# A gated feed-forward kernel with a convolution in front: phases of three rounds in place of two

## The chip, the cores and the metric

The kernel runs on one core of a Trainium2 chip. A core has five engines that run side by side, each with its own queue of instructions, taken in order: TensorE (PE in the profile; PEld is its loading of weights), VectorE (DVE), ScalarE (ACT), GpSimd (POOL) and SyncE (SP), which here only issues transfers. Transfers run on 16 DMA engines, which are shared by a hardware queue (fed by SyncE) and a software queue (fed by GpSimd). SBUF is the working memory. PSUM holds the results of matmuls; the kernel uses it as four buffers of two banks, taken in turn.

The metric is the time of one execution on the device in microseconds (us), as the median of several runs.

## The reference

The input `x` has 8 sequences of 3904 tokens with 192 channels. First comes a causal convolution with 7 taps, separately for each channel: the 192 channels form 8 heads of 24, and all channels of a head share the head's taps, a softmax over `weight[h, :]`. The result, seen as 31232 tokens of 192 channels, goes through a feed-forward block:

```
a = x @ w1          # 192 -> 1024
b = x @ w2          # 192 -> 1024
h = (a * b) @ w3    # 1024 -> 1024
out = h @ w_out     # 1024 -> 192
```

There is no nonlinearity after the product `a * b`, so `w3 @ w_out` is one matrix of 1024 x 192, which the kernel computes once.

## The kernel before

**Rounds.** The tokens are two halves of 15616 (`NS = 2`, `r` = 0 and 1). A round `R` is 512 tokens of each half; there are 31 rounds (0 to 30), the last 256 wide. `first_product(R)` computes for each of 8 f-tiles (128 of the 1024 columns) `pa = x w1` and `pb = x w2` of both halves: six pairs of matmuls, a pair being the two halves on the two halves of the array's rows. ScalarE copies `pa` to SBUF (L564), VectorE multiplies with `pb` (L566) and writes `abT`. `second_product(R, r)` multiplies `abT` by the combined 1024 x 192 matrix (32 matmuls, L582); ScalarE copies the result to a slot `osb` (L587), and SyncE sends it out (L592), 384 KB. `abT` has three buffers.

**Phases.** After a beginning with the first products of rounds 0, 1 and 2, the loop at L795 walks over phases. Phase 0 has no first products; phase p has those of rounds 2p+1 and 2p+2, and then the four second products of rounds 2p and 2p+1. One round is thus always left over, and the last phase has three rounds of second products. All engines' instructions are in the order of this program; nothing is reordered later.

**The convolution** is done in two ways.
- By TensorE, for most rounds: windows of 32 rows of `x` (`xb`, loaded by GpSimd in `x_jobs`, L157) are multiplied by a band matrix (`conv`, L323); the results are evicted (L332), stored to a table `rows` in DRAM (`store`, L354 and L361, on SyncE), and read back by DMA transposes into a ring `xT` of four rounds (`transposes`, L395, on SyncE). This goes by batches of windows; batch 4 covers rounds 5 and 6, batch 5 rounds 9 to 12, batch 6 rounds 17 to 20, batch 7 rounds 25 to 28. A batch is cut into units (`units`: two for batch 4, four for each later one), and `places` says after which of a phase's second products a unit is put.
- By VectorE for the six round pairs in `SIDE` (rounds 7 and 8, 13 and 14, 15 and 16, 21 and 22, 23 and 24, 29 and 30): GpSimd casts the raw channels into a table `rows_c` (`side_cast`, L439), SyncE transposes them (`side_transpose`, L449), ScalarE scales by one tap (`side_first`, L455), and VectorE adds the six others one after another (`side_sums`, L473), writing `side`. A task is 64 channels of a round pair; a step of a task is a unit, and a unit is two instructions where a sequence begins inside the pair. `room` says how many units a phase takes. Two tasks are given to GpSimd in steps (`pool_sums`, L500 to L520).

**Pacing.** GpSimd's loads and steps in a phase stand in `jobs` and `pool_at`; they are put at `points`, pairs of a round's number in the phase and an f-tile. At a point GpSimd first copies two elements of that f-tile's `abT` (L805), and so waits for VectorE.

**SyncE's order around phase 0 and 1:** transposes for sums of the next phase, outputs, the store of a batch when its last unit is done, outputs, and at the end of a phase the transposes into the ring for rounds whose batch is stored (`due`, at most two rounds a phase).

Of the kernel before, what the change touches and what calls it, by code (L numbers as in the profile page):

```python
# [9 lines left out]
BF16 = mybir.dt.bfloat16  # L10
# [6 lines left out]
def kernel(  # L17
# [19 lines left out]
    NS = 2  # L37
    TS = B * S // NS
    CH = 512
    NR = -(-TS // CH)  # L40
    RING = 4 * CH
    LAG = 2
    Q = 64
    NP = D // Q
    C = 32
# [6 lines left out]
    XN = 20 * D  # L52
# [14 lines left out]
    conv_rounds = [R for R in range(NR) if phase_of(R) not in SIDE]  # L67
# [22 lines left out]
    stage = ctx.enter_context(tc.tile_pool(name="stage", bufs=2))  # L90
    work = ctx.enter_context(tc.tile_pool(name="work", bufs=2))
# [8 lines left out]
        return psum.tile([128, 16, 128], BF16, tag="banks", name=name)  # L100

    def slot(shape, dtype, name):
        return stage.tile(shape, dtype, tag="slot", bufs=4, name=name)

    rows = dram.tile([TS, NP * NS * Q], BF16, name="rows")
    rows_c = dram.tile([TS, NP, NS * Q], BF16, name="rows_c")
# [29 lines left out]
    def x_jobs(b, part):  # L136
        js = parts_of(b)[part]
        n, m, E = shape_of(b)
        tiles = xb_of.setdefault(b, {})

        def alloc():
            xb = work.tile([128, XN], BF16, tag="xb", bufs=6, name="xb")
            xb = xb[:, 0:len(js) * m * D].rearrange("p (w d) -> p w d", d=D)
            for j in js:
                tiles[j] = (xb, (j - js[0]) * m)
                for e in range(E):
                    for u in range(m):
# [243 lines left out]
    def transposes(R, first=0):  # L391
        t0, t1 = max(R * CH, first), min((R + 1) * CH, TS)
        a = ring_of[R] * CH % RING + t0 - R * CH
        for k in range(NP):
            nc.sync.dma_start_transpose(  # L395
                out=xT[k][:, a:a + t1 - t0], in_=rows[t0:t1, k * 128:(k + 1) * 128])
# [36 lines left out]
    def side_cast(i, task=None):  # L433
        p, k = task or tasks[i]
        t0, t1 = side_span(p)

        def job(r):
            def run():
                nc.gpsimd.dma_start(  # L439
                    out=rows_c[t0 - HALO:t1, k, r * Q:r * Q + Q],  # L440
                    in_=x_rows[r * TS + t0 - HALO:r * TS + t1, k * Q:k * Q + Q])
            return run
        return [job(r) for r in range(NS)]
# [232 lines left out]
        swap_w(k, HC + 256, DFF, P)  # L676
    load_w3(0, 4, range(2, 4))

    phases = [()] + [(R, R + 1) for R in range(LAG + 1, NR, 2)]
    assert phases[-1][-1] == NR - 1  # L680

    places = {0: (1, 2), 1: (2,), 2: (0, 1, 2), 5: (0, 2), 6: (0, 2), 9: (0, 2), 10: (0, 2)}
    starts, chain, room, p = {}, {}, 0, -1
    for i, (q, k) in enumerate(tasks):
        for cost, f in side_sums(i):
            while room < cost:
                p += 1
                room = 6 if p == 0 else 8 if len(places.get(p, ())) == 2 else 7
                at, ends = 0, {}
                starts.setdefault(p, [])  # L690
            if not chain or chain[max(chain)][-1][0] != i:
                starts[p].append(i)
                n = max(p == 0, -(-ends.get(i - 2, 0) // 2))
                chain.setdefault(p, []).append((i, n, lambda i=i: side_first(i)))
            assert p < q
            room, at = room - cost, at + cost
            chain.setdefault(p, []).append((i, None, f))
        ends[i] = at
# [23 lines left out]
    def later_loads():  # L722
        nc.gpsimd.tensor_scalar(out=taps, in0=taps, scalar1=total, scalar2=None, op0=ALU.mult)
        load_x(3)
        load_wo()
        load_w3(4, 2)
        load_w3(6, 2)
        for i in starts[0]:
            for f in side_cast(i):
                f()  # L730
        load_x(4)
        for i in starts[1]:
            for f in side_cast(i):
                f()
        for f in x_jobs(5, 0):
            f()

    first_product(0, {
        0: seq((swap_w, 1, 256, HC, A, (1,))),
# [19 lines left out]
             for n in [max(v for v in (2, 4) if v * shape_of(b)[1] * G <= CH)]  # L759
             for h in range(0, H, n)]  # L760
    assert sum(map(len, places.values())) == len(units)
    jobs = {p: [] for p in range(1, len(phases))}
    for p, b, part in ((1, 5, 1), (3, 6, 0), (4, 6, 1), (7, 7, 0), (8, 7, 1)):
        jobs[p] += x_jobs(b, part)
    pool_at = {3: 4, 4: 3, 5: 4, 6: 3, 7: 4, 8: 3, 9: 4, 10: 3}
    halves = [(q, k, h) for q, k in BY_POOL for h in range(2)]
    pool_sum = [f for v in halves for f in pool_sums(*v)]
    assert sum(pool_at.values()) == len(pool_sum)
    pool_from = {2: halves[0], 4: halves[1], 6: halves[2], 8: halves[3]}
    casts = [(p - 1, f) for p in starts if p > 1 for i in starts[p] for f in side_cast(i)]  # L770
    casts += [(p, f) for p, t in zip((2, 6), BY_POOL) for f in side_cast(None, t)]
    casts.sort(key=lambda c: c[0])
    for p in jobs:
        due_now = sum(d <= p for d, _ in casts)
        ahead = max(due_now, min(len(casts), 6 - len(jobs[p])))
        jobs[p] = ([f for _, f in casts[:due_now]] + jobs[p] +
                   [f for _, f in casts[due_now:ahead]])
        del casts[:ahead]
    points = ((0, 1), (0, 3), (0, 5), (0, 7), (1, 2), (1, 4))
    sent = [LAG + 3]  # L780
    due = []

# [8 lines left out]
                sent[0] += 1  # L791

    pace = const.tile([1, 2], BF16)
    done = 0
    for p, rounds in enumerate(phases):  # L795
        todo = jobs.pop(p, [])

        each = -(-len(todo) // len(points))
        at = [[todo.pop(0) for _ in range(min(each, len(todo)))] for _ in points]
        for v in {0: (), 2: (1, 4), 3: (0, 2, 4), 4: (0, 1, 3, 4)}[pool_at.get(p, 0)]:  # L800
# [12 lines left out]
        assert not todo  # L813
        for b in {u[0] for u in units[:3]}:
            for xb, p0, w in zero_rows.pop(b, []):
                nc.gpsimd.memset(xb[p0:p0 + PAD, w, :], 0.0)
        for i in starts.get(p + 1, ()):
            side_transpose(i)
        if p == 0:
            pool_tiles()  # L820
        if p in pool_from:
            pool_transpose(*pool_from[p])
        state = set()
        last = NR if p == len(phases) - 1 else done + 2
        seconds = [(R, r) for R in range(done, last) for r in range(NS)]
        done = last
        for n, (R, r) in enumerate(seconds):
            side_steps(p, n, state)
            (last_product if (R, r) == (NR - 1, NS - 1) else second_product)(R, r)
            if n in places.get(p, ()):  # L830
                convolve(p)
        assert len(state) == len(chain.get(p, ()))
        for R in due[:2]:
            transposes(R)
        del due[:2]
    assert not pool_sum and not units and not due and not jobs and done == NR and sent[0] == len(conv_rounds)


# [28 lines left out]
```

## Time and profile before

| | |
|---|---|
| median of 3 runs | 514.11 us (513.78 to 514.99) |
| profiled execution | 514.66 us, span 513.0 us |
| TensorE busy | 506.8 us, 99% of the span |
| VectorE busy | 432.4 us, 84% |
| ScalarE busy | 351.6 us, 69% |
| GpSimd busy | 162.8 us, 32% |
| products on VectorE (L566) | 240 of 1221 ns |
| copies on ScalarE (L564) | 244 of 1012 ns |
| software queue (GpSimd) | 17.07 MB, 36.2% of 16 engines' span |
| hardware queue (SyncE) | 41.39 MB, 37.7% |

The page of a profile gives busy times and shares, the span in 40 slices, the chain of work that ended last, and the costliest groups of instructions. A line of a timeline gives start, duration, engine, source line, operation, tile and count; a bracket gives the idle time before it and what ended it. Durations of neighbouring instructions of one engine can overlap a little, so the distance between two starts is the better cost of one in a row.

### The profile page before, as it was taken

How to read it: one execution, taken by the hardware profiler on the slowest of the kernel's cores; microseconds unless marked ns; L12 is line 12 of the kernel's file. 1: busy time of each engine (PE TensorE's matmuls, PEld its weight loads, DVE VectorE, ACT ScalarE, POOL GpSimd, SP SyncE). 2: the span in 40 equal slices, each digit the busy share in tenths (PEclk: the TensorE clock that was granted, in tenths of full speed). 3: DMA queues.
4: the chain of work that ended last, by engine and by line, in shares of the span. 5: the costliest groups of instructions: out<-in, count | busy, mean ns of one | idle time of the engine just before them, and what ended most of it. 6: DMA issues, size and time to landing. Idle time of an engine off the chain costs nothing.

```text
span 513.0 us, 13921 instructions
## 1 busy us (share of the span) xinstructions
PE 506.8 (99%) x5892; PEld 332.9 (65%) x5892; DVE 432.4 (84%) x430; ACT 351.6 (69%) x397; POOL 162.8 (32%) x243
## 2 busy tenths in 40 slices
PE   8999999999999999999999999999999999999997
PEld 4446846757558585675856758567585675846777
DVE  7898779899798998989989899898998989877380
ACT  6886668677874757777787475777777757476562
POOL 9965031030480724708247072560500000000000
PEclk9999999999999999999999999999999999999999
DMA  9999999895898935956589893584028452210305
GB/s 144 146 162 171 166 110 228 126 175 95 142 193 172 138 80 82 86 145 44 94 152 175 184 139 76 98 48 141 1 64 145 115 148 42 70 57 1 124 3 155
DMA packets 154134, 59.45 MB, mean 116 GB/s; under 512 B 108891, under 2 KB 154071, under 8 KB 154071
## 3 DMA queue, kind: packets, MB, share of 16 engines
q1 hardware_dynamic: 86999, 41.39, 37.7%
q0 software_dynamic: 66912, 17.07, 36.2%
q8 instruction: 46, 0.75, 0.6%
q14 instruction: 17, 0.14, 0.1%
q10 hardware_dynamic: 160, 0.10, 0.1%
HBM read 34.42 MB, written 34.88 MB: 135 GB/s over the span
## 4 chain that ended last, share of the span: by engine, by line
PE 97%; DVE 1%; ACT 1%; issue 1%
PE ops L582 32%; PE pa L557 31%; PE pb L557 30%; PE cps L323 2%; PE wps L650 1%; PE warm L233 1%; ACT asb L564 1%; DVE abT L566 0%; ACT convo L332 0%; PE ops L603 0%; PE tps L385 0%; PE tps L370 0%; DVE xT L377 0%; DVE xb L277 0%; DVE Aband L287 0%
## 5 line engine op out<-in xcount | busy, mean ns | idle before, releaser
L566 DVE TENSOR_TENSOR abT<-asb,pb 128x1024 bf16<-128x1024 bf16 x240 | 292.7, 1221 | 56.7 <-ACT asb L564 41.5
L564 ACT CAST asb<-pa 128x1024 bf16<-128x1024 f32 x244 | 247.0, 1012 | 63.2 <-PE pa L557 62.8
L557 PEld LDWEIGHTS <-wn 64*128 64x128 bf16 x1488 | 138.1, 94 | 84.8 <-issue 2.2
L557 PEld LDWEIGHTS <-ws 64*128 64x128 bf16 x1488 | 130.9, 94 | 71.1 <-issue 0.5
L582 PE MATMUL ops<-W_sb,abT 128*128 128x192 bf16 x1936 | 164.9, 246 | 1.2 <-issue 1.2
L582 PEld LDWEIGHTS <-abT 128*128 128x128 bf16 x1936 | 158.2, 98 | 9.5 <-issue 9.4
L557 PE MATMUL pb<-xT,wn 64*128 64x512 bf16 x456 | 123.9, 376 | 0.0
L557 PE MATMUL pa<-xT,wn 64*128 64x512 bf16 x456 | 123.0, 376 | 0.2
L557 PE MATMUL pa<-xT,ws 64*128 64x512 bf16 x456 | 123.1, 376 | 0.0
L557 PE MATMUL pb<-xT,ws 64*128 64x512 bf16 x456 | 122.0, 376 | 0.0
L587 ACT COPY osb<-ops 128x768 f32<-128x768 f32 (+1 forms) x61 | 48.4, 793 | 86.3 <-PE ops L582 86.3
L473 DVE SCALAR_TENSOR_TENSOR acc<-raw,wC,acc 128x320 f32<-128x320 bf16 (+4 forms) x90 | 76.2, 894 | 0.7
L557 PE MATMUL pb<-side,wn 64*128 64x512 bf16 (+1 forms) x288 | 74.9, 367 | 0.0
L557 PE MATMUL pa<-side,ws 64*128 64x512 bf16 (+1 forms) x288 | 74.4, 367 | 0.0
L557 PE MATMUL pa<-side,wn 64*128 64x512 bf16 (+1 forms) x288 | 74.4, 367 | 0.0
L557 PE MATMUL pb<-side,ws 64*128 64x512 bf16 (+1 forms) x288 | 73.8, 367 | 0.0
L805 POOL COPY pace<-abT 1x2 bf16<-1x2 bf16 x55 | 9.6, 175 | 187.0 <-DVE abT L566 186.9
L500 POOL TENSOR_SCALAR tmp<-acc,wC 128x512 f32<-128x512 bf16 x24 | 37.6, 1568 | 0.8
L332 ACT CAST convo<-cps 128x640 bf16<-128x640 f32 (+2 forms) x58 | 33.8, 659 | 1.8 <-PE cps L323 1.7
L157 POOL DMA_DIRECT2D xb<-in_x_dram x46 | 31.0, 675 | 9.5 <-issue 4.8
L439 POOL DMA_DIRECT2D rows_c<-in_x_dram x36 | 28.5, 792 | 5.4 <-issue 4.4
L520 POOL TENSOR_TENSOR acc<-acc,tmp 128x512 f32<-128x512 f32 (+6 forms) x25 | 26.0, 1047 | 1.7
(72 smaller groups left out, 170.3 us busy)
## 6 DMA issues: line engine op xcount, KB each, us to landing
out_dram<-osb SPq DMA_DIRECT2D x54, 384.0 KB
xb<-in_x_dram POOLq DMA_DIRECT2D x28, 240.0 KB, 7.1
rows_c<-in_x_dram POOLq DMA_DIRECT2D x30, 130.0 KB, 4.1
out_dram<-osb SPq DMA_DIRECT2D x12, 192.0 KB
rows<-convo SPq DMA_DIRECT2D x9, 240.0 KB
xb<-in_x_dram POOLq DMA_DIRECT2D x8, 228.0 KB, 7.9
rows<-convo SPq DMA_DIRECT2D x9, 150.0 KB
w3b<-in_moe_w_dram POOLq DMA_DIRECT2D x4, 256.0 KB, 5.4
```

Of the source, the lines that this page charges most:

```text
L157: nc.gpsimd.dma_start(out=tiles[js[0]][0][group(r, e), s:s + w, :], in_=bass.AP(tensor=x.tensor, offset=(r * TS + t - PAD) * D, ap=[[D, C] ...
L323: nc.tensor.matmul(o.rearrange("p (w g) -> p w g", g=wd)[:, :, c - c0:c1 - c0], Aband[group(r, e), h, :], xb[group(r, e), s:s + m, c:c1], ...
L332: f(out=convo[:, e::E, k, :, lo:lo + c] .rearrange("p w r g -> p r w g"), in_=src[:, :, :, o:o + c])
L439: nc.gpsimd.dma_start(out=rows_c[t0 - HALO:t1, k, r * Q:r * Q + Q], in_=x_rows[r * TS + t0 - HALO:r * TS + t1, k * Q:k * Q + Q])
L473: nc.vector.scalar_tensor_tensor(out=side_of[p][:, k, 0:t1 - t0] if last else a, in0=raw[:, HALO + lo - t0 - d:HALO + hi - t0 - d], scalar ...
L500: nc.gpsimd.tensor_scalar(out=out, in0=pool_raw[0][:, HALO - d:HALO - d + CH], scalar1=wC[:, k, K - 1 - d:K - d], scalar2=None, op0=ALU.mult)
L520: nc.gpsimd.tensor_tensor(out=a, in0=a, in1=tmp[:, lo - t0:hi - t0], op=ALU.add)
L557: nc.tensor.matmul(p[:, r, f * N:f * N + N], w_of(i, k, r)[rs, ft * 128:(ft + 1) * 128], operand(R, k, rs), start=(k == 0), stop=(k == NP ...
L564: nc.scalar.copy(out=asb[:, :, 0:per * N], in_=pa[:, :, 0:per * N])
L566: nc.vector.tensor_tensor(out=ab[:, f0, :, 0:N], in0=asb[:, :, 0:N], in1=pb[:, :, 0:N], op=ALU.mult)
L582: nc.tensor.matmul(ops[:, g // 2, (g % 2) * D:(g % 2) * D + D], ab[:, jt, r, g * 128:(g + 1) * 128], W_sb[:, jt, :], start=(jt == 0), stop ...
L587: nc.scalar.copy(out=osb.rearrange("p (a g) d -> p a (g d)", g=2), in_=ops[:, 0:ng // 2, 0:2 * D])
```

## The change

Phases now have three rounds. Phase 0 has the second products of rounds 0, 1 and 2; phase p (1 to 8) has the first products of rounds 3p, 3p+1 and 3p+2, and then the second products of the same three. Phase 9 has the first products of 27 to 29 and the second products of 27; phase 10 the first product of 30 and the second products of 28, 29 and 30. What hangs on the phases is dealt out anew:

- `room` becomes 9 units in phase 0 and 12 in the others (6, and 7 or 8, before), and the first product that needs a sum is found by `stage_of`.
- `places` puts the convolution units elsewhere: batch 4 in phase 0, all four units of batch 5 in phase 1, batch 6 in phases 2 and 3, batch 7 in phases 5 and 6. The units of a phase's sums are asked for after each second product instead of ahead of it.
- `later_loads` no longer loads the first half of batch 5, but casts for the tasks that start in phases 0, 1 and 2 (six tasks in all, three before); both halves of batch 5 are loaded in phase 1.
- GpSimd's steps go to phases 2 to 6 (3, 4, 7, 7, 7), and a phase has eight points.
- The transposes into the ring are issued at the end of a phase for every stored round needed up to two phases later.
- There are six output slots instead of four, and five `xb` buffers instead of six.

```diff
+    TRIO = LAG + 1
...
-        return stage.tile(shape, dtype, tag="slot", bufs=4, name=name)
+        return stage.tile(shape, dtype, tag="slot", bufs=6, name=name)
...
-            xb = work.tile([128, XN], BF16, tag="xb", bufs=6, name="xb")
+            xb = work.tile([128, XN], BF16, tag="xb", bufs=5, name="xb")
...
-    phases = [()] + [(R, R + 1) for R in range(LAG + 1, NR, 2)]
...
-    places = {0: (1, 2), 1: (2,), 2: (0, 1, 2), 5: (0, 2), 6: (0, 2), 9: (0, 2), 10: (0, 2)}
+    trios = [tuple(range(R, R + TRIO)) for R in range(0, NR - 1, TRIO)]
+    assert trios[-1][-1] == NR - 2
+    phases = [((), trios[0])] + [(t, t) for t in trios[1:-1]] + \
+        [(trios[-1], trios[-1][:1]), ((NR - 1,), trios[-1][1:] + (NR - 1,))]
+
+    def stage_of(R):
+        return R // TRIO
+
+    places = {0: (0, 2), 1: (1, 2, 3, 4), 2: (3, 5), 3: (1, 3), 5: (3, 5), 6: (1, 3)}
...
-                room = 6 if p == 0 else 8 if len(places.get(p, ())) == 2 else 7
+                room = 9 if p == 0 else 12
...
-            assert p < q
+            assert p < stage_of(2 * q + 1)
...
-        for i in starts[1]:
+        for i in starts[1] + starts[2]:
             for f in side_cast(i):
                 f()
-        for f in x_jobs(5, 0):
-            f()
...
+    points = ((0, 1), (0, 4), (0, 7), (1, 2), (1, 5), (2, 0), (2, 3), (2, 6))
     jobs = {p: [] for p in range(1, len(phases))}
-    for p, b, part in ((1, 5, 1), (3, 6, 0), (4, 6, 1), (7, 7, 0), (8, 7, 1)):
+    for p, b, part in ((1, 5, 0), (1, 5, 1), (2, 6, 0), (2, 6, 1), (4, 7, 0), (5, 7, 1)):
         jobs[p] += x_jobs(b, part)
-    pool_at = {3: 4, 4: 3, 5: 4, 6: 3, 7: 4, 8: 3, 9: 4, 10: 3}
+    pool_at = {2: 3, 3: 4, 4: 7, 5: 7, 6: 7}
...
-    points = ((0, 1), (0, 3), (0, 5), (0, 7), (1, 2), (1, 4))
...
-        last = NR if p == len(phases) - 1 else done + 2
-        seconds = [(R, r) for R in range(done, last) for r in range(NS)]
-        done = last
-        for n, (R, r) in enumerate(seconds):
-            side_steps(p, n, state)
+        side_steps(p, 0, state)
+        for n, (R, r) in enumerate((R, r) for R in ends for r in range(NS)):
             (last_product if (R, r) == (NR - 1, NS - 1) else second_product)(R, r)
+            side_steps(p, n + 1, state)
             if n in places.get(p, ()):
                 convolve(p)
...
-        for R in due[:2]:
-            transposes(R)
-        del due[:2]
+        while due and stage_of(due[0]) <= p + 2:
+            transposes(due.pop(0))
```

More of the change, by code (lines that the diff above doesn't have):

```diff
@@ L677 @@
     load_w3(0, 4, range(2, 4))
-    phases = [()] + [(R, R + 1) for R in range(LAG + 1, NR, 2)]
-    assert phases[-1][-1] == NR - 1
-    places = {0: (1, 2), 1: (2,), 2: (0, 1, 2), 5: (0, 2), 6: (0, 2), 9: (0, 2), 10: (0, 2)}
+    trios = [tuple(range(R, R + TRIO)) for R in range(0, NR - 1, TRIO)]
[5 more added lines that the diff above has]
+    places = {0: (0, 2), 1: (1, 2, 3, 4), 2: (3, 5), 3: (1, 3), 5: (3, 5), 6: (1, 3)}
     starts, chain, room, p = {}, {}, 0, -1
@@ L768 @@
     assert sum(pool_at.values()) == len(pool_sum)
-    pool_from = {2: halves[0], 4: halves[1], 6: halves[2], 8: halves[3]}
-    casts = [(p - 1, f) for p in starts if p > 1 for i in starts[p] for f in side_cast(i)]
-    casts += [(p, f) for p, t in zip((2, 6), BY_POOL) for f in side_cast(None, t)]
+    pool_from = {1: halves[0], 3: halves[1], 4: halves[2], 5: halves[3]}
+    casts = [(p - 1, f) for p in starts if p > 2 for i in starts[p] for f in side_cast(i)]
+    casts += [(p, f) for p, t in zip((1, 4), BY_POOL) for f in side_cast(None, t)]
     casts.sort(key=lambda c: c[0])
@@ L774 @@
         due_now = sum(d <= p for d, _ in casts)
-        ahead = max(due_now, min(len(casts), 6 - len(jobs[p])))
+        ahead = max(due_now, min(len(casts), len(points) - len(jobs[p])))
         jobs[p] = ([f for _, f in casts[:due_now]] + jobs[p] +
@@ L793 @@
     pace = const.tile([1, 2], BF16)
-    done = 0
-    for p, rounds in enumerate(phases):
+    for p, (rounds, ends) in enumerate(phases):
         todo = jobs.pop(p, [])
@@ L799 @@
         at = [[todo.pop(0) for _ in range(min(each, len(todo)))] for _ in points]
-        for v in {0: (), 2: (1, 4), 3: (0, 2, 4), 4: (0, 1, 3, 4)}[pool_at.get(p, 0)]:
+        for v in {0: (), 3: (1, 3, 5), 4: (0, 2, 4, 6), 7: range(7)}[pool_at.get(p, 0)]:
             at[v].append(pool_sum.pop(0))
@@ L813 @@
         assert not todo
-        for b in {u[0] for u in units[:3]}:
-            for xb, p0, w in zero_rows.pop(b, []):
+        for b in list(zero_rows):
+            for xb, p0, w in zero_rows.pop(b):
                 nc.gpsimd.memset(xb[p0:p0 + PAD, w, :], 0.0)
@@ L832 @@
         assert len(state) == len(chain.get(p, ()))
-        for R in due[:2]:
-            transposes(R)
-        del due[:2]
-    assert not pool_sum and not units and not due and not jobs and done == NR and sent[0] == len(conv_rounds)
+        while due and stage_of(due[0]) <= p + 2:
+            transposes(due.pop(0))
+    assert not pool_sum and not units and not due and not jobs and sent[0] == len(conv_rounds)
 _INS = ['x', 'weight', 'moe_w1', 'moe_w2', 'moe_w3', 'moe_w_out']
```

## The prediction

> **What bounds the kernel now.** I read the page first (busy shares, slices, chain), then the chain in order of time, then the timelines of the DMA queue of SyncE, of VectorE and of GpSimd, and last the two DMA queues in short windows. All times are of the profiled execution: 514.66 us with a span of 513.0 us, so 1.66 us lie around the span. It is 0.55 us above the median of three runs (514.11 us).
>
> ```profile
> span 513.0 us, 13921 instructions
> ...
> PE 506.8 (99%) x5892; PEld 332.9 (65%) x5892; DVE 432.4 (84%) x430; ACT 351.6 (69%) x397; POOL 162.8 (32%) x243
> ...
> DMA  9999999895898935956589893584028452210305
> ...
> PE 97%; DVE 1%; ACT 1%; issue 1%
> ```
>
> TensorE is the bound: 99% busy, and 97% of the chain is its own work. Only 6.2 us of the span are without a matmul, so no reordering can win much. But the DMA engines are just as full in the first eight slices (to about 103 us), and lighter later: what must arrive early has no room there.
>
> ```profile
> 63.99 1.15 issue
> 65.14 0.82 PE ops L582 x8
> 65.96 0.75 PE pa L557 x6
> ...
> 130.79 0.75 PE pa L557 x6
> 131.54 0.65 PE pb L557 x6
> ...
> 151.62 10.67 PE ops L582 x128
> 162.28 0.75 PE pa L557 x6
> ```
>
> The chain gives the size of a phase: from 130.79 to 162.28 is 31.49 us. An f-tile of a first product is two groups of 0.648 us, 1.296 us; 16 of them are 20.73. Second products come as 2.75 us for 32 matmuls and 5.39 for 64 elsewhere in this chain: 0.0825 us a matmul and 0.11 for the start, so 10.67 for 128. What is left is 0.10 us, in the first group (0.75 for 0.65). One change from first to second products and back thus costs 0.21 us. The 1.15 us at 63.99 is the only real hole.
>
> ```profile
> 49.63 3.10 SPq L361 DMA_DIRECT2D rows<-convo  x8
> 56.36 0.31 SPq L354 DMA_DIRECT2D rows<-convo  x1
> 57.76 11.46 SPq L395 DMA_TRANSPOSE xT<-rows  x6
> 69.34 5.11 SPq L449 DMA_TRANSPOSE raw<-rows_c  x4
> 74.54 1.82 SPq L592 DMA_DIRECT2D out_dram<-osb  x3
> 76.46 10.87 SPq L361 DMA_DIRECT2D rows<-convo  x8
> 87.86 0.30 SPq L354 DMA_DIRECT2D rows<-convo  x1
> 88.68 0.39 SPq L592 DMA_DIRECT2D out_dram<-osb  x1
> 89.72 7.98 SPq L395 DMA_TRANSPOSE xT<-rows  x6
> ```
>
> This is SyncE's queue, in order and nearly without a pause from 57.76 to 97.7. The last line transposes rounds 5 and 6 into the ring. Round 5 needs the first three of the six: issued at 89.72, 90.91 and 92.54, ready at about 93.8. The first product of round 5 begins at 97.91. So 4.1 us are to spare here, the shortest margin that I found.
>
> **The change, part by part.**
>
> Fewer changes between products. Before there are 14 phases with first products, after it 10: 4 x 0.21 = 0.84 us off TensorE. The matmuls are the same 5892. The tail is the same: rounds 28, 29 and 30 still have all 160 matmuls of their second products after the last first product. Taken: -0.8.
>
> Round 5 is needed earlier. Phase 1 is now rounds 3, 4 and 5. Phase 0 has 64 more matmuls (5.28 us), so phase 1 begins at 65.96 + 5.28 = 71.24, and round 5 after two rounds (2 x 10.37 + 0.10 = 20.83) at 92.07, 5.84 us earlier than now. Its way is: convolution of batch 4 in phase 0 (now after the first and third second product, for the second and third; the last still ends near 61.9), its rows stored (L361, L354), and the transposes. In SyncE's order the same three outputs come before the store, but three outputs instead of one between the store and the transposes. An output is 384 KB: alone in the last phases some 1.33 us at 290 to 325 GB/s, so two more are 2.7 us in the same queue. GpSimd's loads share the DMA engines; the view by queue, its columns packets, MB and share of 16 engines:
>
> ```profile
> q0 software_dynamic: 416, 0.16, 63.8%
> q1 hardware_dynamic: 416, 0.31, 63.3%
> ```
>
> In these two microseconds (from 82) the software queue and SyncE's moved packet for packet the same. Now batch 5's first half is loaded before phase 0's products, and its second half with two casts from 70.6 to 79.7: 960 + 260 = 1220 KB beside the store. After the change all of batch 5 is loaded in phase 1, paced by VectorE's products: casts (260 KB) at about 75.7, then pairs of 480 KB at about 79.6, 83.5 and of 456 at 87.4 and 91.3. Up to 87.4 that is again 1220 KB, so I take the same delay as now: ready at 93.8 + 2.7 = 96.5, and 4.4 us of waiting at 92.07.
> Bounds: low, with no loads in the way, three outputs 4.0 + store (half of the 10.9 us that a batch of twice the size takes at 386.3, alone) 5.5 + three outputs 4.0 + three transposes 4.1 (1.36 each when alone) from 74.54 gives 92.1, a wait of 0. High, with all packets issued until 91 counted (1040 a cast, 640 or 608 a load, one for each row moved): 2080 + 3776 = 5856 against the 3283 that the software queue moved from 74 to 90; 2570 more, at the 416 a microsecond of both queues together, are 6.2 us: ready at 102.7, a wait of 10.6.
> [...]
>
> TensorE after such a wait. The only start from rest in this trace is at 1.04, where nine warm-up matmuls of 3456 columns took 3.06 us; at the later 0.0825 us per 192 columns they would take 1.49. So a restart costs between 0 and 1.6 us; I take the middle, 0.8, since a wait of 4 us lies between the hole of 1.15 us, after which nothing was slow (16 f-tiles at 1.296), and a start from nothing.
> [...]
>
> VectorE's sums. The sums run while TensorE does second products. Per phase now 12 units in a window of 192 x 0.0825 + 0.11 = 15.95 us (plus 0.46 for each convolution unit: a phase with two lasts 32.42). A unit that crosses a sequence start costs 1.35 (57.23 to 63.96 is five), a plain one 1.21:
>
> ```profile
> 255.33 1.29 DVE L473 SCALAR_TENSOR_TENSOR side<-raw,wC,acc 128x1024 bf16<-128x1024 bf16 x1
> 256.54 1.21 DVE L473 SCALAR_TENSOR_TENSOR acc<-raw,wC,acc 128x960 f32<-128x960 bf16 x1
> ...
> 260.51 2.46 DVE L566 TENSOR_TENSOR abT<-asb,pb 128x1024 bf16<-128x1024 bf16 x2 [1.24 <-ACT asb L564]
> ```
>
> The tightest new phase is 4 (rounds 12 to 14): ten crossing units and two plain, 15.9 us, no convolution: it just fits. Here VectorE had 1.24 us to spare before its next product. Taken: 0; if the units cost their full durations (1.49 and 1.285), 17.5 us, less some 0.3 us that the banks of PSUM let TensorE run ahead: 1.2 us. The other phases have 13 to 16 us of sums beside 16 to 18: hidden.
>
> Others, taken at nothing. Task 1 of the sums is cast and transposed before phase 0 (two casts on GpSimd, two transposes of 1.25 us on SyncE): SyncE is idle from 46.2 to 49.63, and casts issued at 36.4 land like the neighbours there, 8 us later; batch 4's loads then land by about 51.5 for a convolution at 55.2. If that cover went, ScalarE would stand in front of its first sums and outputs: up to 3 us. Four convolution units in phase 1: ScalarE has 4 x (0.8 + 2.1) + 1.15 = 12.8 us for 12.4 us of TensorE, covered by two free banks: 0 to 0.5. Six output slots for six outputs; without them ScalarE would wait for SyncE, which reaches the first output at 74.5. GpSimd's seven steps in phases 4 to 6 take 0.17 + 0.78 + 1.57 + 1.27 = 3.8 us each, and its points come every 3.9.
>
> Sum: 514.66 - 0.8 + 4.4 + 0.8 = 519.1; less 0.55 for the median, **518.5 us**.
>
> **The rivals.**
> A, the forecast: round 5 waits for its transposes. A wait of 1 us without a restart gives 514.3, 10.6 with 1.6 gives 525.5; 515.5 to 523 holds most of it.
> B, the other side: the transposes are in time, and the change does what it says. This needs a wait under about 1 us, so ready by 93. For it: the loads before phase 0's products are 180 KB lighter (four of 240 KB fewer, six casts of 130 KB more), the store of batch 3 (landed only at 64.86, when the transposes of round 4 go on) could land 2 us sooner, and the loads in phase 1 begin 5 us later than now. Against it: two more outputs in the same queue. Time 514.1 - 0.8 = 513.3; if the hole of 1.15 goes as well, 512.2.
> C: VectorE is the bound in phase 4, 1.2 us there and nothing elsewhere: 514.5.
> D: batch 5 is late at its first unit in phase 1, at 92.07 + 10.46 + 5.4 = 107.9. The last large pair is issued at 91.3 to 92.7, and pairs now take 6.1 to 13.1 us: 98.8 to 105.8; the small pair at 95.2 some 10 us: 105.2. It decides if they are 2 to 3 us later than that; 3 us late gives 516.3.
>
> **How the numbers follow.** A 0.50 (slower 0.48, same 0.02), B 0.32 (faster 0.21, same 0.11), C 0.08 (slower 0.04, same 0.04), D 0.10 (slower 0.09, same 0.01). 0.2% is 1.03 us, about what a measurement here can tell from no change. Faster 0.21, same 0.18, slower 0.61. A gives the predicted time. The range reaches down to B with the hole gone, 512.2, and up to 523: A's own range is 515.5 to 523.
>
> **What would show it.** A: in the chain a hole before the first group of the third round of phase 1, near 92 to 97, released by a DMA into xT, and groups longer than 0.65 us right behind it if the restart costs. In SyncE's timeline the transposes of round 5 issued behind three outputs, after 90. B: no hole, and phases of 31.1 + 15.95 + 0.1 = 47.2 us. C: a hole of about 1 us at the start of phase 5, released by a VectorE product. D: convolution matmuls in phase 1 that wait for a load. Wrong altogether would be a hole elsewhere, such as in phase 0 in front of the convolutions.

## The result, and the profile after

The changed kernel takes 532.19 us (median of 5, 530.48 to 534.11) against 514.11 us before (median of 5, 513.54 to 514.99): a ratio of 1.0352, with an interval of 1.0322 to 1.0383. It is slower by the mechanism that was forecast, but by 18 us where 4.4 were forecast, and outside the range. The profiled execution took 533.05 us, with a span of 531.3 us against 513.0. Ratios compare the executions that lie up to 1.5% above the fastest of their kernel.

From the page of the kernel after:

```profile
span 531.3 us, 13894 instructions
...
PEclk9999999589999999999999999999999999999999
DMA  9999979923899955599957934322760340140024
```

A slice is 13.3 us. In the eighth (93 to 106 us) the granted clock of TensorE is low (0.55 over the slice), and the ninth still shows 8 (0.81); nowhere else is it low. In finer windows it is 1.00 until 94 us, 0.67 from 94 to 95, 0.50 from 95 to 111.4, and 0.99 from 111.4 to 112. The DMA engines are full in the seventh and eighth slices (a 9 each) and at two and three tenths in the two behind them. The timeline of TensorE, at the start of the third round of phase 1 (start, duration, engine and line; the bracket is the idle time before it and what ended it):

```profile
90.68 0.38 PE L558 MATMUL pb<-xT,wn 64*128 64x512 bf16 x1
100.57 0.60 PE L558 MATMUL pa<-xT,wn 64*128 64x512 bf16 x1 [9.51 <-DMA xT<-rows]
102.67 0.58 PE L558 MATMUL pa<-xT,ws 64*128 64x512 bf16 x1 [1.49 <-DMA xT<-rows]
105.65 0.58 PE L558 MATMUL pa<-xT,wn 64*128 64x512 bf16 x1 [2.36 <-DMA xT<-rows]
```

Round 4 ends at 91.06, when the last of these matmuls of `pb` does, and nothing held it up. Round 5 then waits three times, once for each of its transposes: 9.51, 1.49 and 2.36 us. Its first group of `pb` comes at 106.03 where 91.71 was due, 14.3 us late. Right behind it the chain of waits shows groups of six matmuls:

```profile
107.54 1.28 PE pa L558 x6
...
112.10 0.65 PE pa L558 x6
```

These groups take twice the usual time until 111.4; the rest of the round has the usual 0.65. The whole round from 106.03 lasts 12.55 us in place of 9.72: 2.8 us more.

SyncE's queue in the same stretch:

```profile
68.65 5.12 SPq L450 DMA_TRANSPOSE raw<-rows_c  x4
73.86 1.97 SPq L593 DMA_DIRECT2D out_dram<-osb  x3
...
84.69 3.25 SPq L593 DMA_DIRECT2D out_dram<-osb  x3
88.42 14.69 SPq L396 DMA_TRANSPOSE xT<-rows  x6
```

The transposes for rounds 5 and 6 are issued at 88.42, when the part of batch 4's store that they need has landed, and even before the 89.72 of the kernel before. Yet the first of them lands 12 us later, and the six take 14.7 us to issue and not 8. From the issue of the first to the landing of round 5's third it is 17.2 us. In the kernel before it was 5.5: the trace has the last completion signal of that transpose at 95.2 us (93.8, which the prediction took for it, is the end of its issue).

The two DMA queues show what else was at work; their view gives packets, MB and share of 16 engines. In the kernel after from 98 to 100 us, while round 5 is transposed:

```profile
q0 software_dynamic: 536, 0.20, 102.4%
q1 hardware_dynamic: 504, 0.12, 81.6%
```

In the kernel before from 94 to 96 us, while it transposes rounds 5 and 6:

```profile
q1 hardware_dynamic: 1042, 0.25, 56.0%
```

Before, GpSimd's queue was empty by then, and SyncE's moved 1042 packets in 2 us. After, GpSimd's loads of batch 5 are at work, and in this window the two queues move about the same number of packets, 536 and 504, together as many as SyncE's had alone. A transpose's packets are small (0.12 MB in 504, some 240 bytes), so at these rates a transpose of 128 KB (512 tokens of 128 channels), which needed 1 us of these engines in the kernel before, needs 2 in the kernel after, by estimate. The landings show it: 2.1 us from the first to the second, 3.0 to the third.

The whole crowd, from 74 us to the landing of round 5's last transpose, in the kernel after (to 105.65):

```profile
q0 software_dynamic: 7296, 2.21, 70.3%
q1 hardware_dynamic: 7412, 3.90, 65.7%
```

and in the kernel before (to 95.2):

```profile
q1 hardware_dynamic: 5980, 3.02, 69.1%
q0 software_dynamic: 3283, 1.06, 58.9%
```

So after it is 2.03 MB more, 1.15 of GpSimd's and 0.88 of SyncE's, and the landing is 10.4 us later. At the mean rate of before (4.08 MB in 21.2 us) 2.03 MB take 10.5 us. Counted in packets it is 5445 more, 12.5 us at the rate of before. What was moved until the landing thus accounts for the delay, and bytes do it no worse than packets. The rate is a mean: in five of the kernels below it is 164 to 201 GB/s until round 5's landing, for 194 here. Nor is the flow even: from 96 to 98 us the two queues moved only 0.15 MB, where it was 0.42 in the two us ahead; no run here shows why.

A second loss lies at the ends of phases 2 and 5. ScalarE, at the change from phase 2 to 3:

```profile
184.99 1.95 ACT L333 CAST convo<-cps 128x320 bf16<-128x320 f32 x4
186.79 3.05 ACT L565 CAST asb<-pa 128x1024 bf16<-128x1024 f32 x3
```

A convolution unit is the last thing of these phases (`places` 5), and ScalarE evicts its four results just as the first `pa` of phase 3 is ready at about 185.3. Its copies begin at 186.79, and TensorE stands for want of a free buffer. Phases 3 and 6 last 49.49 us each (phase 6 from its first matmul at 329.24 to the next phase's at 378.73).

The account of the 18.3 us of span:

| | us |
|---|---|
| fewer changes between products | -0.8 |
| the hole of 1.15 us in phase 0 is not there in this execution; phase 1 begins at 70.23 for 71.24 | -1.0 |
| round 5 waits | +14.3 |
| groups at half speed behind the wait | +2.8 |
| a unit waits for ScalarE in phase 1 | +0.2 |
| convolution units at the ends of phases 2 and 5, 1.38 each | +2.8 |
| sum | 18.3 |

The 0.8 is read from the phases that nothing disturbs: 378.80 to 425.99 to 473.12, 47.2 us for three rounds. The 1.38 is 49.49 less the 48.11 that the same phases take in the third experiment below.

### The profile page after: what moved, and what is told of

It is laid out like the page before. It is cut to its first block, busy times and chain, and to the rows that moved or that the text cites. A ratio compares the mean times of both kernels' runs of the same rounds, so it can differ in the third digit from the quotient of the medians.

```text
span 531.3 us, 13894 instructions
## 1 busy us (share of the span) xinstructions
PE 511.7 (96%) x5892; PEld 342.0 (64%) x5892; DVE 432.0 (81%) x430; ACT 351.1 (66%) x397; POOL 161.4 (30%) x232
## 4 chain that ended last, share of the span: by engine, by line
PE 89%; DMA 4%; ACT 3%; SPq 2%; DVE 1%; issue 1%; DVEq 0%
PE ops L583 30%; PE pa L558 28%; PE pb L558 28%; DMA xT<-rows 2%; DMA rows<-convo 1%; PE cps L324 1%; ACT convo L333 1%; SPq L396 1%; PE wps L651 1%; ACT asb L565 1%; DVE abT L567 1%; PE warm L234 1%; SPq L362 1%; DMA out_dram<-osb 0%; ACT osb L588 0%
## 5 line engine op out<-in xcount | busy, mean ns | idle before, releaser
L567 DVE TENSOR_TENSOR abT<-asb,pb 128x1024 bf16<-128x1024 bf16 x240 | 292.2, 1220 | 70.0 <-ACT asb L565 38.6
L558 PE MATMUL pa<-xT,wn 64*128 64x512 bf16 x456 | 125.4, 381 | 12.4 <-DMA xT<-rows 11.9
L558 PE MATMUL pb<-xT,wn 64*128 64x512 bf16 x456 | 126.3, 380 | 1.2 <-DVE abT L567 1.0
L558 PE MATMUL pa<-xT,ws 64*128 64x512 bf16 x456 | 125.5, 381 | 1.5 <-DMA xT<-rows 1.5
L808 POOL COPY pace<-abT 1x2 bf16<-1x2 bf16 x44 | 7.7, 174 | 178.3 <-DVE abT L567 178.2
```

What stands on the lines that cost most here:

```text
L558: nc.tensor.matmul(p[:, r, f * N:f * N + N], w_of(i, k, r)[rs, ft * 128:(ft + 1) * 128], operand(R, k, rs), start=(k == 0), stop=(k == NP ...
L567: nc.vector.tensor_tensor(out=ab[:, f0, :, 0:N], in0=asb[:, :, 0:N], in1=pb[:, :, 0:N], op=ALU.mult)
```

## The experiments

The open question of the wait: why so much longer than 4.4 us? Theory L: the loads of batch 5, now all in phase 1, hold the transposes up. Theory Q: it is the order of SyncE's queue, outputs ahead of the transposes. Beside these, U: the unit at the end of phases 2 and 5 costs 1.4 us each time; and the slow groups come from the clock, or else from something that the wait leaves behind, such as late operands. All edits are against the changed kernel, and ratios against the kernel before in the same series. What is read from a trace is one execution each.

**The first half of batch 5 loaded before phase 0, as in the kernel before.**

```diff
             for f in side_cast(i):
                 f()
+        for f in x_jobs(5, 0):
+            f()
...
-    for p, b, part in ((1, 5, 0), (1, 5, 1), (2, 6, 0), ...
+    for p, b, part in ((1, 5, 1), (2, 6, 0), ...
```

> The changed kernel with one part undone: the first half of batch 5 (four loads of 240 KB) is loaded before phase 0's products again, as in the kernel before, so that phase 1 has only the second half and two casts beside the outputs and the transposes of round 5. Theory L (the loads that run beside SyncE's queue hold the transposes up): in the changed kernel the third transpose of round 5 landed at 105.6, and the loads of phase 1 up to then are some 1900 KB; half of them gone should bring it to about 99 or 100, TensorE's wait from 14.3 to about 8 us, and the time from 532.2 to 524 to 527. Theory Q (the outputs queued ahead decide, loads hardly matter): no more than 2 us, 530 or above.

Measured: 527.02 us, ratio 1.0239 (1.0214 to 1.0264), 5 us less. The first wait falls from 9.51 to 6.71 us, the second is 1.91, and the last transpose lands at about 101.5. The time is the upper end of theory L's 524 to 527, and Q's 530 is out. But four loads fewer in phase 1 leave two thirds of round 5's wait (8.6 of 13.4 us in the profiled execution, the longest of the four with 529.09 us). The loads crowd what is ahead instead: the four transposes for the sums, ahead of everything in SyncE's queue, now take 7.65 us to issue in place of 5.12, and round 3 waits 1.22 us for its transposes at the start of phase 1.

**Round 5's transposes ahead of the last three outputs.**

```diff
             if n in places.get(p, ()):
                 convolve(p)
+                while due and due[0] == 5:
+                    transposes(due.pop(0))
```

> The changed kernel with the transposes of round 5 issued right behind the store of batch 4, ahead of the last three outputs of phase 0; nothing else moves. Theory Q (the three outputs of 384 KB between store and transposes hold round 5 up): the transposes start at about 85 to 86 without outputs in the queue ahead of them, the third lands at about 91 to 95, TensorE waits 0 to 4 us and its clock stays up: 515 to 520. Theory L (the loads beside them decide): the transposes still stretch to 2 or 3 us each, the third lands after 98, and the time is 523 to 528.

Measured: 527.32 us, ratio 1.024 (1.020 to 1.028), also 5 us less. Q alone had 515 to 520 and is out; the size is that of L (523 to 528). SyncE's queue, and then TensorE's timeline, of this kernel:

```profile
84.71 3.75 SPq L396 DMA_TRANSPOSE xT<-rows  x3
```

```profile
98.09 0.58 PE L558 MATMUL pa<-xT,wn 64*128 64x512 bf16 x1 [3.13 <-DMA xT<-rows]
```

Issued at 84.71 with nothing behind the store in front of them, the three land at 91.64, 94.34 and 98.09: 2.7 and 3.75 us apart, with the loads beside them. The first lands 8.9 us sooner than in the changed kernel, the last 7.6, and so Q has a share; the slow landing remains, and it is the loads'. This profiled execution (523.99 us) is the shortest of four, the others lie from 526.45 to 528.54, so its waits (6.2 us together) are at the low end.

**The units one product earlier in phases 2 and 5.**

```diff
-    places = {..., 2: (3, 5), 3: (1, 3), 5: (3, 5), 6: (1, 3)}
+    places = {..., 2: (2, 4), 3: (1, 3), 5: (2, 4), 6: (1, 3)}
```

> The changed kernel with the convolution units of phases 2 and 5 behind the third and fifth second product in place of the fourth and sixth, so that none stands right ahead of the next first product. Theory E (a unit at the end of a phase leaves ScalarE its evictions just when the first copies of the next phase are due; the phases after 2 and 5 measured 49.4 us for 48.1): 2 x 1.3 us less, 529.0 to 530.3 against the changed kernel's 532.2. Rival (those two phases are longer because of the sums' order or the loads): no change within 0.5 us.

Measured: 529.22 us, ratio 1.0287 (1.0259 to 1.0315), 3.0 us less. Phases 3 and 6 fall to 48.11 us (182.00 to 230.11, 325.41 to 373.52): 2.8 us together. U is shown, with its size. This trace has something else: after nearly the same wait for round 5 (9.30, 1.54 and 1.54 us) the groups are slow for only 2.7 us behind the last landing, at 104.42, and not for 5.7, and the loss is 1.3 us.

**TensorE kept busy through the wait**, with 60 matmuls on zeros ahead of round 5, whose result nobody uses.

```diff
+            if R == 5:
+                warm(60)
             first_product(R, ...)
```

> The changed kernel with 60 matmuls of zeros (512 columns, 0.216 us each, 12.9 us) put ahead of the first product of round 5, where TensorE waits 14.3 us for its transposes. They do no work of the output. Theory C (the slow groups behind the wait, 1.28 us for 0.65 over some 5.5 us, come from the clock that falls in an idle array): the groups stay at 0.65, the granted clock stays 1.0, and the time falls by 2 to 2.8 us, to about 529.5 to 530. Rival (the groups are slow because the transposes and loads that land then disturb TensorE's reads): groups behind the dummy matmuls still take 1.28, time unchanged or up to 1 us longer.

Measured: 529.27 us, ratio 1.0287 (1.0270 to 1.0304), 2.9 us less. The chain of waits of this kernel:

```profile
90.81 13.06 PE warm L234 x60
103.87 0.75 PE pa L558 x6
```

The groups behind it have 0.65 us from the first on, the granted clock is 0.999 over the span where it was 0.984, and the slice that held a 5 holds a 9. So the slow groups are the clock's answer to the idle time, and not something that late transfers do to TensorE. The medians agree with the 2.8 us that the timeline gave; the two profiled executions lie 4.25 us apart, since round 5 also began some 1.4 us sooner here.

**All loads of batch 5 before phase 0**, with two of the edits above (transposes ahead of the outputs, units earlier). What is left of L would go by this. The rival, S: the loads then crowd phase 0's own transposes and the store, and all comes later.

```diff
+        load_x(5)
...
-    for p, b, part in ((1, 5, 0), (1, 5, 1), (2, 6, 0), ...
+    for p, b, part in ((2, 6, 0), ...
...
-        ahead = max(due_now, min(len(casts), ...))
+        ahead = due_now if p == 1 else max(due_now, min(len(casts), ...))
```

> The changed kernel with three edits: all of batch 5 is loaded before phase 0's products, right behind the casts there (phase 1 keeps only two casts), the transposes of round 5 go ahead of the last three outputs of phase 0, and the units of phases 2 and 5 stand one second product earlier. GpSimd's queue left the DMA engines free from 66 to 78 in the changed kernel, so the loads should land by about 70. Theory L+Q (loads and outputs together make all of the wait): store of batch 4 landed by about 82 to 84, transposes of 1.3 us each, round 5 ready by 88 to 90, no wait at 91; then 0.8 us of changes between products and the hole of 1.15 us in phase 0 remain as the gain: 512 to 513.5, faster than the kernel before by 0.1 to 0.4%. Rival S (SyncE's own issue and the store of batch 4 are too slow even so, or the loads now delay the transposes of rounds 3 and 4): a wait of 2 to 5 us remains there or at round 4, 515 to 520.

Measured: 522.31 us, ratio 1.0162 (1.0132 to 1.0192). SyncE's queue of this kernel:

```profile
68.05 8.99 SPq L450 DMA_TRANSPOSE raw<-rows_c  x4
...
92.57 3.74 SPq L396 DMA_TRANSPOSE xT<-rows  x3
```

The sums' transposes take 9 us to issue in place of 5, the outputs and the store behind them some 3 us more, and so round 5's come out 8 us later than with the loads in phase 1. They then land fast (1.2 and 1.4 us apart; waits of 3.90, 0.78 and 0.80 us). S is right in kind, though the time lies above its 515 to 520: the crowd is moved, not removed.

**The same with round 5's transposes behind the outputs again.** Against the kernel before this one:

```diff
-                while due and due[0] == 5:
-                    transposes(due.pop(0))
```

> The same without the edit of the transposes: they stand behind the three outputs again. Measures what the outputs cost when no load runs beside them. Theory: outputs alone take 1.33 us each, so round 5 is ready about 4 us later than with the transposes first, at 91 to 94 for a need at 91: 0 to 3 us of wait, 512 to 516.5. Rival (outputs slow the queue far more than their bytes, as the 12 us of the first transpose suggested): wait of 5 us and more, above 518.

Measured: 524.83 us, ratio 1.0209 (1.0177 to 1.0242); the first wait is 6.22 us and not 3.90. So the rival is right, and the place of the outputs is worth 2.5 us by the medians here, where it was 5 with the loads in phase 1. (The profiled executions lie 1.9 us apart, and 0.9 of that is a later start of phase 1.)

With the changed kernel and the second experiment this makes four combinations. From the issue of round 5's first transpose to the landing of its third it is 17.2 us with loads beside and outputs ahead (88.42 to 105.65), 13.4 with the loads alone (84.71 to 98.09), 6.5 with the outputs alone (93.90 to 100.37), and 5.3 with neither (92.57 to 97.82). So it is mainly the loads that make the transposes slow; moving them ahead gains little because the issue then comes later.

**Half of batch 5 early, transposes first, units earlier**: the first three edits together.

```diff
+        for f in x_jobs(5, 0):
+            f()
...
+                while due and due[0] == 5:
+                    transposes(due.pop(0))
...
+    places = {..., 2: (2, 4), 3: (1, 3), 5: (2, 4), 6: (1, 3)}
```

> The same as the first of these three, but only the first half of batch 5 is loaded early; the second half stays in phase 1, beside the store and the transposes. Theory L+Q: three or four loads of 240 KB still run beside the transposes, which take 2 us instead of 1.3; round 5 ready at 91 to 94, a wait of 0 to 3 us: 512.5 to 517. Rival (each edit takes the same part of the wait away): the two edits together give 527.0 and 527.3 less 532.2 twice, so about 522, less 2.9 for the units: 519 to 520.

Measured: 519.08 us, ratio 1.0089 (1.0053 to 1.0124). The three gains alone sum to 13 us and this is 13.1 below the changed kernel: by the medians they add up, as the rival had it. But the executions lie between 516.70 and 523.26 us, and in the profiled one, the longest, the waits left are 0.68, 2.06 and 1.52 us; its sums' transposes begin at 69.85 and need 8 us to issue. Every way of shifting loads leaves the queue's first members, the transposes for sums, in front of a store that is urgent. So the next edit shifts these.

**The sums' transposes of phase 0 to its end**, with round 5's ahead of the outputs and the units earlier. The loads stay in phase 1.

```diff
-        for i in starts.get(p + 1, ()):
+        for i in starts.get(p + 1, ()) if p else ():
             side_transpose(i)
...
             transposes(due.pop(0))
+        for i in starts.get(p + 1, ()) if not p else ():
+            side_transpose(i)
```

> The changed kernel with three edits, the loads left as the change has them: the four transposes for phase 1's sums (5.1 us of SyncE ahead of the first output, at 68.6) go to the end of phase 0, behind the ring's; the transposes of round 5 go ahead of the last three outputs; the units of phases 2 and 5 one second product earlier. Theory O (what SyncE's queue puts between the transposes of round 4 and those of round 5 decides, all of it together): outputs and store of batch 4 begin 5 us earlier, before any load of phase 1 is issued; the store lands by about 78 to 80, the third transpose of round 5 by 84 to 87, need at 91: no wait, no fall of the clock. What is left is the gain of the fewer changes between products and the hole in phase 0: 512 to 513.5. Rival B (the DMA engines are full in any order until some 95): as when the loads were moved ahead, a wait of 3 to 5 us and 518 to 522.

Measured: 515.29 us, ratio 1.0013 (0.9998 to 1.0029). SyncE's queue of this kernel:

```profile
77.39 4.21 SPq L396 DMA_TRANSPOSE xT<-rows  x3
```

7.3 us earlier than with the transposes ahead of the outputs alone. Round 5 does not wait, and the granted clock is 1.0: theory O is right about the wait, and B is out. But the time is above O's 512 to 513.5. A new wait stands in phase 2, in the chain:

```profile
148.88 11.68 DMA xb<-in_x_dram
...
160.60 0.36 PE cps L324 x17
```

Batch 6's last load, issued by GpSimd at 148.35 behind its steps of a sum, lands at 160.56, and its unit, now one product earlier, waits 1.3 us for it; ScalarE's evictions then come close to the end of the phase again. Phase 2 lasts 50.2 us (119.24 to 169.45) in place of 48.1. Against the changed kernel the span is 17.8 us less: 14.3 + 2.8 + 2.8, less these 2.1.

**The same with round 5's transposes behind the outputs.**

```diff
-                while due and due[0] == 5:
-                    transposes(due.pop(0))
```

> The same without the edit of round 5's transposes: they stand behind the last three outputs. Theory O: the outputs of 384 KB take 1.33 us each alone and up to 2.7 beside loads, so round 5 is ready 4 to 8 us later than with the transposes first, at 88 to 95 for a need at 91: 512 to 518. Rival B: 522 or above, no better than the run with the transposes first alone (527.3) less the 2.9 us of the units.

Measured: 521.74 us as the median of nine executions, which lie unusually far apart, from 514.99 to 524.36 us. The ratio is 1.0087 (1.0052 to 1.0123), of five of them; median over median is 1.014. In the profiled one (521.74 us) round 5 waits 2.47, 3.39 and 0.17 us. The median is above O's 512 to 518 and just below B's 522, so neither forecast holds as it stands. Both places in SyncE's queue matter: the waits sum to 13.4 us with both as in the changed kernel, 6.2 with only the outputs moved back, 6.0 with only the sums' transposes moved back, 0 with both (one execution each, that with 6.2 the shortest of its four; the units of phases 2 and 5 do not touch this). By the medians, moving the outputs alone is worth 4.9 us, moving the sums' transposes alone 7.5 (529.22 to 521.74, the units earlier in both), and both together 13.9 (529.22 to 515.29), with the new wait of phase 2 in it. Why the executions scatter so is open.

**Phase 2's units after the fourth and fifth product**, to give batch 6's load the time.

```diff
-    places = {..., 2: (2, 4), ...
+    places = {..., 2: (3, 4), ...
```

> The run with the sums' transposes later, the transposes of round 5 first and the units earlier took 515.29 us with no wait for round 5, but phase 2 was 50.2 us long for 48.1: its first convolution unit, moved ahead by one second product, stood waiting 1.3 us for batch 6's loads. Here the units of phase 2 stand behind the fourth and fifth second product, 2.6 us later for the first, still not at the phase's end. Theory: the loads, landed at 160.6 there, just make 161; phase 2 falls to about 48.1, the time to 513.2 to 513.8, which leaves the gain of the changes between products against the kernel before (514.1 to 514.5). Rival: the loads are issued behind GpSimd's steps and later still, the wait stays: 515.

Measured: 513.74 us, ratio 0.9991 (0.9977 to 1.0005), as expected. The chain of this kernel has no piece that isn't TensorE's at the end of phase 2:

```profile
150.99 10.67 PE ops L583 x128
...
167.86 0.75 PE pa L558 x6
```

Phase 2 is at 48.11 us, the span at 511.9 us, and no wait of TensorE from phase 0 to phase 3 is over 0.25 us. This is phases of three rounds as the change wants them, and it cannot be told from the kernel before.

**Batch 6's first half loaded in phase 1** instead, with phase 2's units after the third and fifth product, as in the kernel of 515.29 us. Against that kernel:

```diff
-    for p, b, part in (..., (2, 6, 0), (2, 6, 1), ...
+    for p, b, part in (..., (1, 6, 0), (2, 6, 1), ...
```

> The same run with the units left behind the third and fifth second product, and the first half of batch 6 loaded at the end of phase 1 in place of phase 2. Theory: the last load of batch 6 is then issued two points (7.8 us) earlier, the unit does not wait: 513.2 to 513.8 as well. Rival: the loads in phase 1 hold up what SyncE moves there, the transposes of the sums or the store of batch 5, and the gain is lost: 515 or above.

Measured: 514.66 us, ratio 1.0013 (0.9997 to 1.0028); the median is 0.9 us above the run before and lies between the theory's 513.8 and the rival's 515. Batch 6 is in time, but more loads in phase 1 stand beside the sums' transposes that were moved there: in the profiled execution (517.25 us, the longest of twelve) one of these takes 11.13 us to land, until 111.3, ScalarE stands in front of its first step of that sum, and the convolution unit behind it waits 1.4 us and a second product 1.2.

## Why the prediction was wrong in size

**The mechanism (A).** Right: round 5 of phase 1 waits for its transposes, in the place named, released by a DMA into `xT`, with groups longer than 0.65 us behind it. That it was due at 92.07 was right too: it was 91.06, and the 1.0 us is the hole in phase 0, which did not occur here.

**The size of the wait.** The step that failed is "Up to 87.4 that is again 1220 KB, so I take the same delay as now: ready at 93.8 + 2.7 = 96.5". It was 105.65. Three things are in that step.
- The loads. The same bytes were loaded beside the *store* as before, but the step that counts is the transposes, and these had run after the loads. The prediction's own list had a pair at 87.4 and one at 91.3, each with some 10 us to land. Until round 5 was ready GpSimd's queue moved 1.15 MB more than before; at the mean rate of the crowd, 0.193 MB a microsecond, that is an estimate of 6.0 us, where the sum had nothing.
- The outputs. SyncE's queue moved 0.88 MB more, most of it the two outputs; by the same estimate that is 4.6 us, where the sum had 2.7 at the rate of outputs alone.
- The start. The 93.8 is the end of an issue and not a landing, which came at 95.2. Issue to landing is 2.7 us a transpose even with no load beside (92.57 to 95.24 with all loads early). So 2.7 us were to spare before, and not 4.1.

Together these are 9.3 us (6.0, 1.9 and 1.4), and the landing came 9.1 us later than the 96.5.

The low bound had the transposes alone as well. Its high bound, a wait of 10.6 us, took the 416 packets a microsecond of both queues together from 82 to 84 and counted all that GpSimd's queue would move, which was right in kind, but it left out the pair forecast at 91.3 (issued at 90.73, landing 13.9 us later): 7296 of its packets were moved before round 5 was ready, not 5856.

How the two queues shared the DMA engines differs from window to window of the crowd in the kernel after. GpSimd's and SyncE's packets are nearly equal in several, 420 and 412 from 92 to 94, 217 and 215 from 96 to 98, 536 and 504 from 98 to 100, and far apart in others, 658 and 185 from 84 to 86, 318 and 592 from 90 to 92. Whether one queue was without work for a part of these, the view does not tell, and no run here shows what sets the shares.

**The restart.** 0.8 us taken, 0 to 1.6 as bounds, 2.8 measured in the profiled execution. The reason for the middle was that a wait of 4 us lies between a hole of 1.15 us and a start from nothing; a wait in three pieces of 13.4 us is beyond that, and the upper bound, from the nine first matmuls of the program, was too low for this execution. It would have held for the 1.3 us with the units earlier. The experiment with dummy matmuls shows that it is the clock: 0.999 over the span for 0.984, and groups of 0.65 us. While the granted clock was 0.50 the groups took 1.28 us in place of 0.65. The slow stretch behind the last landing was 5.7 us here (waits of 9.51, 1.49 and 2.36 us), 2.7 with the units earlier (9.30, 1.54 and 1.54), and 2.8 with the transposes first (0.8, 2.3 and 3.1). So the waits do not give its length by their sum, and no run here shows what does.

**Not in the sum at all:** the convolution units at the ends of phases 2 and 5, 2.8 us. The prediction counted ScalarE's work for the units of phase 1 alone, and said nothing of those of phases 2 and 5. In the kernel before no unit of a phase with first products came after the last of its four second products; a unit in that place puts 1.95 us of evictions between the last second product and the first copy.

**Fewer changes.** Right: 0.8 us, 47.2 us a phase as stated under B.

**B** (in time, 513.3 us, 512.2 without the hole) was wrong of the changed kernel, but its figure was that of the idea: with the queue put in another order and the units of phases 2 and 5 moved, the kernel takes 513.74 us.

**C** (VectorE the bound in phase 4) did not happen: second products of 15.95 us and the next first group straight behind, at 281.30. Taken at nothing, and rightly.

**D** (batch 5 late at its first unit) did not happen, and not only because the wait of round 5 gave the load time: in the kernels of 515.29 and 513.74 us, where round 5 does not wait, no unit of phase 1 waits for a load either. The same kind came one batch on, with the unit of phase 2 moved ahead: batch 6, 1.3 us.

**Four units in phase 1**, 0 to 0.5 us: 0.2.

**Where the gain went.** There was little of it, 0.8 us of 514, and the price was paid in a stretch where the DMA engines have little free (a 9 each for the seventh and eighth slices of the kernel after). What is open: the hole of about 1 us in phase 0. It is 1.15 us before, absent after, 1.09 in the kernel with all loads early and the outputs first, 0.21 in the best one. Its cause was not tried. Nor was the deferral of the sums' transposes tried with everything else as in the changed kernel.

## What to carry to other kernels

When a transfer is moved to where another queue is at work, count what both queues move until the transfer that matters has landed, and not only what its own queue has more in front: here 2.03 MB at the 0.193 MB a microsecond of the crowd give the 10.4 us of delay, where two outputs at their rate alone gave 2.7. Count to the landing and not to the end of the issue. In a queue that is taken in order, as SyncE's is here, look for what is urgent and what is merely early; two groups of transfers, worth 4.9 and 7.5 us, stood ahead of the urgent one, and putting both behind it was worth more than any shift of the loads. And work of another stage does not belong between the last product of one phase and the first copy of the next: a convolution unit there cost 1.38 us each time.

## What was not expected of the hardware

- Transposes that land 1.2 and 1.4 us apart when the other queue is empty took 2.1 to 3.75 us beside loads (the kernel after, and the transposes first). From 98 to 100 us the queues moved packets of some 240 bytes (transposes) and some 380 (loads) nearly one for one, 504 and 536. The first transpose landed 2.7 us after its issue with neither loads beside nor outputs ahead, 6.9 with loads (84.71 to 91.64), and 12.2 with both.
- A wait in three pieces with one pair of matmuls between them left TensorE at half its clock (0.50 granted, groups of 1.28 us) for 5.7 us of work in one execution, a loss of 2.8 us, and after nearly the same wait for 2.7 us in another, a loss of 1.3; 60 matmuls on zeros kept the clock up (0.999 over the span).
- Loads put earlier can make a later transfer later still: with all of batch 5 ahead of phase 0, four transposes took 9.0 us to issue in place of 5.1.
